# A fused retention and SwiGLU kernel: other places for the first weight loads and for one value load, and the first group's down-projection in three passes over w_out

## The chip, the cores and the metric

The kernel runs on one core of one Trainium2 chip. The metric is the device time of one execution in microseconds (us). The engines of the core have each an instruction queue that is worked off in order: TensorE (PE, with its weight loads shown apart as PEld), VectorE (DVE), ScalarE (ACT), GpSimd (POOL) and SyncE (SP). Transfers are issued from the queues of GpSimd, SP and ScalarE and are carried out by 16 DMA engines. PSUM, which TensorE writes, has eight banks, numbered 0 to 7 here.

## What is computed

`q`, `k` and `v` are (4, 8, 768, 64): batch, heads, positions, head width. The first half is a recurrent retention, the second a feed-forward block on its output, with 512 = 8 x 64 features per token, 3072 tokens and 1536 hidden features.

```python
gamma = 1.0 - 2.0 ** (-5.0 - np.arange(H))
for t in range(S):
    state = gamma[None, :, None, None] * state + np.einsum('bhd,bhe->bhde', k[:, :, t], v[:, :, t])
    y[:, :, t] = (1 / np.sqrt(D)) * np.einsum('bhd,bhde->bhe', q[:, :, t], state)
x = y.transpose(0, 2, 1, 3).reshape(B * S, H * D)

xn = x / np.sqrt(np.mean(x * x, axis=-1, keepdims=True) + 1e-6) * rms_g
g = xn @ w_gate
out = (g * (1 / (1 + np.exp(-g))) * (xn @ w_val)) @ w_out
```

Inputs and output are float32.

## The kernel before

The 768 positions are cut into six chunks of 128. In each chunk the four batches make two pairs, 0 and 1. The recurrence is done chunk by chunk: inside a chunk as a masked product of `q` and `k` (`a_ps`, then `am`) with the values, and across chunks through a state per batch and head. A chunk's rows are normed (`rstd` is a power of the mean square, on GpSimd; `xn` is the normed row), transposed to features by tokens (`xnT`), and go as a group of 512 tokens through the feed-forward: `gv` makes the gate and value products of some of the twelve 128-column blocks of `w_gate` and `w_val`, applies SiLU on ScalarE (`sg`) and multiplies on VectorE into `hT`; `down` multiplies `hT` with the twelve row blocks of `w_out` and stores a batch's 128 rows.

The order of instructions is written out by hand: each engine's queue holds its instructions in the order in which the program names them. TensorE works for the group of one chunk while the attention of the next chunk is put between its blocks.

The start is special, since all weights have to be fetched while the first chunk is computed. Weights, `q` and `k` are converted from float32 to bfloat16 by the transfer itself, and these transfers are issued by GpSimd. `load_w(n0, n1)` (line 83) loads blocks n0 to n1 of both weights as two transfers, `load_pair(c, p, n)` (line 93) one of `q`, `k`, `v` of pair p in two transfers of 64 partitions, `load_wo` (line 88) four row blocks of `w_out`. GpSimd's queue at the start is: `q` and `k` of pair 0, index patterns (lines 133 to 135), the second half of pair 0's `v`, `q` and `k` of pair 1, the positions `pos_p` and `pos_n` (lines 140 to 143), `ya_p` (line 195, from the positions), then blocks 0 and 1, blocks 2 and 3 (lines 569 and 570), the power of pair 0 (line 603), blocks 4 to 7, the decayed values of pair 0 (`vp_pair`, line 608), blocks 8 and 9, and the power of pair 1 (line 633). The `v` of pair 1 is issued from SP (line 587) after the first masked product.

ScalarE's queue there is: eight exponentials for the mask, the cast of pair 0's `v` (`vb`), the decays (`decays`, line 206: `vd_p`, `vd_n`, then `yd_p`, which reads `ya_p`, then `yd_n`), the copy of `g_bc` out of PSUM (line 593), the squares of pair 0 (line 330), two copies of pair 1's transposed `q`, and pair 0's `xn` (line 352). The copies of pair 1's transposed `k` are VectorE's (lines 604 and 605). The cast of pair 1's `v` (line 625) stands between the second and the third block's `sg`.

PSUM banks are given out by `bank` (line 65). Up to the end of chunk 1's start it takes them from a list written by hand (`first`), then from a rotation over eight banks (`order`). Once `split[0]` is true, tiles of the feed-forward turn over banks 4 to 7 and all others over banks 0 to 3. A bank is given to its next tile when the readers of its last tile are done. Before the change `split[0]` becomes true at line 723, ahead of the second group's feed-forward.

The first group's down-projection (lines 682, 692, 693 and 709) runs a batch at a time, twelve matmuls of 512 columns into one bank, with the second chunk's attention between the batches. The end of that stretch reads:

```python
    down(0, 1)
    down(0, 2)
    t_dma(2, 0)
    for n, e in (("q", "a"), ("k", "v")):
        for a in range(2):
            tp(1, 1, n, a, e)
```

and goes on with the transposes and products of pair 1 of chunk 1 (`x_pe`, `ap`), and `down(0, 3)`.

Of the kernel before, what the change touches and what calls it, by code (L numbers as in the profile page):

```python
# [8 lines left out]
F32 = mybir.dt.float32  # L9
# [7 lines left out]
def kernel(  # L17
# [11 lines left out]
    nc = tc.nc  # L29
    ctx.enter_context(tc.manual_schedule())  # L30

    B, H, S, D = q.shape
    C = 128
    NCH = S // C
    NHP = H // 2
    DM = H * D
    DFF = moe_w_gate.shape[1]
    KS = DM // 128
    NFF = DFF // 128
# [5 lines left out]
    work = ctx.enter_context(tc.tile_pool(name="work", bufs=4))  # L45
# [17 lines left out]
    split = [False]  # L63

    def bank(name, dtype=F32, ffn=False, i=None):
        if i is None and split[0]:
            i = turn[ffn] % 4 + 4 * ffn
            turn[ffn] += 1
        elif i is None and first:
            i = first.pop(0)  # L70
        elif i is None:
            i = order[0]
            order.append(order.pop(0))
        return psum.tile([128, 512 if dtype == F32 else 1024], dtype, name=name, tag=f"p{i}")
# [3 lines left out]
    wo_b = const.tile([128, NFF, DM], BF16, name="wo_b")  # L78
# [4 lines left out]
    def load_w(n0, n1, *kinds):  # L83
        sl = slice(n0 * 128, n1 * 128)
        for i in kinds or (0, 1):
            nc.gpsimd.dma_start(out=(wg_b, wv_b)[i][:, :, sl], in_=(wg_v, wv_v)[i][:, :, sl])
# [4 lines left out]
    U = {}  # L91

    def load_pair(c, p, n, batches=(0, 1), eng=None, after=None):
        u = U.setdefault((c, p), {})
        if n not in u:
            if n == "v":
                u[n] = work.tile([128, H, 2 * D], F32, name="v2f", bufs=3)
            else:
                u[n] = work.tile([128, H, 2 * D], BF16, name=n + "2b", bufs=4)
        for b in batches:  # L100
            i = (eng or nc.gpsimd).dma_start(out=u[n][b * 64:b * 64 + 64], in_=pair_v[n][c, 2 * p + b])  # L101
            if after is not None:
                tc.add_manual_dep(i.ins, after.ins.name, SYNC_DEP, reason="transfer order")

    def load(c, b, names="qkv"):
        u = U.setdefault((c, b), {})
        for n in names:
            if n == "v":
                x = work.tile([128, H, D], F32, name="v_f", tag="v_f", bufs=6)
                nc.gpsimd.dma_start(out=x, in_=unit_v[n][c, b])  # L110
            else:
                x = work.tile([128, DM], BF16, name=n + "b", bufs=8)
                nc.gpsimd.dma_start(out=x.rearrange("p (h d) -> p h d", h=H), in_=unit_v[n][c, b])  # L113
            u[n] = x
# [19 lines left out]
    for i in range(2):  # L134
        nc.gpsimd.iota(offp[i * 64:i * 64 + 64], pattern=[[-1, 2], [1, 2], [2, 64]], base=0, channel_multiplier=-2)
    load_pair(0, 0, "v", (1,))
    load_pair(0, 1, "q")
    load_pair(0, 1, "k")
    for i in range(2):
        nc.gpsimd.iota(pos_p[i * 64:i * 64 + 64], pattern=[[C, 2], [1, 2]], base=1, channel_multiplier=2,  # L140
                       allow_small_or_imprecise_dtypes=True)
    nc.gpsimd.iota(pos_n, pattern=[[C, NCH]], base=1, channel_multiplier=1,
                   allow_small_or_imprecise_dtypes=True)

    ones = const.tile([128, 512], BF16, name="ones")
    nc.vector.memset(ones, 1.0)  # L146
# [31 lines left out]
    def mask_exp(a):  # L178
        for i in range(2):
            for x in range(2):  # L180
                nc.scalar.activation(mask0[a][i][:, x], reach, AF.Exp, scale=lng[2 * (2 * a + x) + i], bias=lnscale)
# [39 lines left out]
    def copy(eng, out, in_):  # L221
        return (nc.scalar.copy if eng == "a" else nc.vector.tensor_copy)(out, in_)
# [16 lines left out]
    def tc_(c, p, n, a, eng):  # L239
        u = U[c, p]  # L240
        t = work.tile([128, 2, 2, 2, 64], BF16, name=n + "2T", tag=n + "T", bufs=8)
        copy(eng, t.rearrange("p x b e j -> p (x b e j)"), u["t_ps", n, a][:, :512])
        u[n + "T", a] = t
# [14 lines left out]
    def ap_mask(c, p, a, i):  # L258
        u = U[c, p]
        am = work.tile([128, 2, 2, 128], BF16, name="am2", tag="am", bufs=12)  # L260
        m = mask0[a][i] if c == 0 else causal_p[:, None, :].to_broadcast([128, 2, 256])
        u["mask", a, i] = nc.vector.tensor_tensor(  # L262
            out=am.rearrange("p x e t -> p x (e t)"),
            in0=u["a_ps", a][i].rearrange("p (x t) -> p x t", x=2), in1=m, op=ALU.mult)
        u["am", a, i] = am

    def v_cast(p):
        u = U[0, p]
        u["vb"] = work.tile([128, H, 2 * D], BF16, name="vb", bufs=2)
        nc.scalar.copy(u["vb"], u["v"])  # L270
# [87 lines left out]
    def begin(c):  # L358
        XT[c] = work.tile([128, KS, GT], BF16, name="xnT", bufs=2)
# [18 lines left out]
    def y1(p):  # L378
        u = U[1, p]
        u["y"] = [bank("y_ps") for _ in range(2)]  # L380
        for b in range(2):
            for hp in range(NHP):
                nc.tensor.matmul(u["y"][b][:, hp * 128:(hp + 1) * 128],
                                 u["qT", hp // 2][:, hp % 2, b].rearrange("p e j -> p (e j)"), st_d[p][:, b, hp],
                                 start=hp == 0, stop=False, skip_group_check=True)
        for h in range(H):
            hp, i = h // 2, h % 2
            for e in range(2):
                for b in range(2):
                    r = slice(b * 64, b * 64 + 64)  # L390
                    nc.tensor.matmul(u["y"][b][:, h * D:h * D + D], u["am", hp // 2, i][r, hp % 2, e, :],
                                     u["vp"][r, h, e * D:e * D + D], start=False,
                                     stop=h == H - 1 and e == 1, skip_group_check=True)

    def y1_out(p):
        u = U[1, p]
        x = work.tile([128, 2, NHP, 2, D], F32, name="x", tag="x", bufs=2)
        u["x"] = x.rearrange("p b a i d -> p b (a i d)")
        for b in range(2):
            nc.vector.tensor_tensor(  # L400
                out=u["x"][:, b].rearrange("p (h d) -> p h d", h=H), in0=u["y"][b].rearrange("p (h d) -> p h d", h=H),
                in1=yd_p[:, :, None].to_broadcast([128, H, D]), op=ALU.mult)
# [115 lines left out]
    HT = {}  # L518
# [22 lines left out]
    def store(eng, c, b, m, o_sb):  # L541
        if c < 2:
            for e in range(2):
                eng.dma_start(out=out_e[c, b, e][:, m], in_=o_sb[e * 64:e * 64 + 64, m])
        else:
            eng.dma_start(out=out_v[c, b][:, m], in_=o_sb[:, m])

    def down(c, b):
        ps = bank("o_ps", ffn=True)
        for n in range(NFF):  # L550
            nc.tensor.matmul(ps, HT[c][:, n, b * C:(b + 1) * C], wo_b[:, n, :], start=n == 0, stop=n == NFF - 1)  # L551
        o_sb = work.tile([128, DM], F32, name="o_sb", bufs=3)
        nc.scalar.copy(o_sb, ps)  # L553
        store(nc.sync, c, b, slice(0, DM), o_sb)

    def down_last(c, b):
        o_sb = work.tile([128, DM], F32, name="o_sb", bufs=3)
        for i in range(2):
            m = slice(i * 256, i * 256 + 256)
            ps = bank("o_ps", ffn=True)  # L560
            for n in range(NFF):
                nc.tensor.matmul(ps[:, :256], HT[c][:, n, b * C:(b + 1) * C], wo_b[:, n, m],  # L562
                                 start=n == 0, stop=n == NFF - 1)
            copy("av"[i], o_sb[:, m], ps[:, :256])
            store(nc.scalar if i == 0 else nc.sync, c, b, m, o_sb)


    begin(0)
    load_w(0, 2)
    load_w(2, 4)  # L570

    mask_exp(0)
    mask_exp(1)
    heat(11)
# [9 lines left out]
    for a in range(2):  # L584
        for i in range(2):
            ap_mask(0, 0, a, i)
    load_pair(0, 1, "v", eng=nc.sync, after=U[0, 0]["mask", 0, 0])
    v_cast(0)

    g_ps = bank("g_bc_ps")  # L590
# [11 lines left out]
    eps0(0)  # L602
    power(0, 0)
    tc_(0, 1, "k", 0, "v")
    tc_(0, 1, "k", 1, "v")
    load_w(4, 6)
    load_w(6, 8)
    vp_pair(0, 0)
# [70 lines left out]
    gv(0, 11, 12, 0, GT)  # L679
    load(2, 0)  # L680
    y1(0)
    down(0, 0)
    y1_out(0)
    square(1, 0, 0)
    square(1, 0, 1)
# [3 lines left out]
    load(2, 1)  # L689
    vp_pair(1, 1)  # L690
    load(2, 2)
    down(0, 1)
    down(0, 2)
    t_dma(2, 0)
    for n, e in (("q", "a"), ("k", "v")):
        for a in range(2):
# [9 lines left out]
            ap_mask(1, 1, a, i)  # L706
    load(2, 3)
    t_dma(2, 1)
    down(0, 3)

    def run(steps, after):
        for i, step in enumerate(steps):
# [7 lines left out]

    steps = [L(gv, 1, n, n + 2, t, t + 256) for t in (0, 256) for n in range(0, NFF, 2)]
    steps += [L(down, 1, b) for b in range(B)]
    split[0] = True
    run(steps, {
        0: [L(y1, 1), L(y1_out, 1), L(kvp, 1, 1)],
        1: [L(square, 1, 1, 0), L(square, 1, 1, 1), L(rstd, 1, 1), L(state1, 1)],
# [18 lines left out]
    for c in range(2, NCH):  # L745
# [6 lines left out]
        after = {}  # L752
        if d < NCH:
            after = {
                0: [L(begin, d)],
                1: [L(values, d, 0), L(vp, d, 2), L(vp, d, 3)],
                2: [L(y_out, d, 0, 0)] + [L(load, d + 1, 0)] * more,
                3: [L(y_out, d, 0, 1)] + [L(state_add, d, 0)] * more,
                4: [L(square, d, 0, 0)] + [L(load, d + 1, 1)] * more,
                5: [L(a_pair, d, 1), L(a_mask, d, 2, 0), L(square, d, 0, 1), L(rstd, d, 0)]  # L760
                   + [L(state_cast, 0)] * more,
                6: [L(a_mask, d, 2, 1), L(norm, d, 0, 0), L(x_dma, d, 0, 0)]
# [40 lines left out]
```

## Time and profile before

| what | value |
|---|---|
| median of 13 runs | 239.54 us (238.3 to 247.33) |
| the profiled execution's own time | 238.3 us |
| its span on the core | 236.5 us |
| TensorE busy | 225.2 us, 95% of the span |
| VectorE, ScalarE, GpSimd busy | 54%, 37%, 49% |
| granted TensorE clock | full in every slice |
| read from HBM, written to it | 28.32 MB, 6.29 MB |
| TensorE busy from 17.2 to 22.7 us | 3.93 of 5.50 us |
| TensorE busy from 28.0 to 46.6 us | 18.34 of 18.60 us |
| TensorE busy from 46.6 to 59.3 us | 12.60 of 12.70 us |

A timeline line has the start and the length in us, the engine, the line of the kernel, the operation, what is written and read, how many instructions were merged (x), and in brackets how long the engine was idle before it and what ended that. A line of the chain of waits has start, length and what was running. A line on transfers has what is written and read, the issuing queue, the number of transfers, the size as stored, and the median time from issue to landing. "PE", "DVE", "ACT" and "POOL" are TensorE, VectorE, ScalarE and GpSimd.

### The profile page before, as it was taken

What the parts mean: (1) busy time and instruction counts of PE and PEld (TensorE: products, weight loads), DVE (VectorE), ACT (ScalarE), POOL (GpSimd) and SP (SyncE); (2) the same over time, 40 slices, a digit from 0 to 9 for tenths busy, and PEclk for the clock granted to TensorE, in tenths of its full rate; (3) what the DMA queues carried; (4) which work ended last, traced back from release to release, by engine and by line L of the source; (5) the groups of instructions that cost most, each with busy time, mean ns of one, the idle gap of its engine ahead of it and who ended that gap; (6) DMA issues with size and microseconds to landing.
All of it is one profiled execution on the core that took longest, in us unless ns stands there. A gap on an engine that the chain in (4) does not pass through costs nothing.

```text
span 236.5 us, 5411 instructions
## 1 busy us (share of the span) xinstructions
PE 225.2 (95%) x2198; PEld 137.2 (58%) x2223; DVE 127.7 (54%) x222; ACT 87.5 (37%) x176; POOL 115.7 (49%) x150
## 2 busy tenths in 40 slices
PE   6787999999999999999999999999999999999993
PEld 2455775545898854684544684544674444854443
DVE  3775644827486585736956246957155742243300
ACT  2865634242443333235332325332325241433221
POOL 8976799559699923963918704907001010000000
PEclk9999999999999999999999999999999999999999
DMA  8999999999999999596999994994600205100022
GB/s 104 165 192 200 187 175 183 192 196 228 135 201 154 184 144 186 109 204 89 111 138 170 92 167 131 141 174 111 182 21 0 44 3 162 60 3 0 0 89 90
DMA packets 83306, 30.24 MB, mean 128 GB/s; under 512 B 69521, under 2 KB 78993, under 8 KB 83282
## 3 DMA queue, kind: packets, MB, share of 16 engines
q0 software_dynamic: 51328, 16.52, 67.9%
q1 hardware_dynamic: 31280, 13.25, 30.1%
q8 instruction: 17, 0.28, 0.5%
q10 hardware_dynamic: 674, 0.14, 0.3%
q14 instruction: 7, 0.06, 0.1%
HBM read 28.32 MB, written 6.29 MB: 146 GB/s over the span
## 4 chain that ended last, share of the span: by engine, by line
PE 87%; DMA 5%; DVE 3%; POOL 2%; issue 2%; DVEq 0%; POOLq 0%
PE v_ps L532 25%; PE o_ps L551 25%; PE g_ps L532 25%; DMA wv_b<-in_moe_w_val_dram 3%; DMA k2b<-in_k_dram 2%; PE y_ps L505 2%; PE a_ps L460 2%; DVE am L262 1%; PE y_ps L489 1%; PE t_ps L234 1%; PE o_ps L562 1%; PE kv_ps L498 1%; PE a_ps L255 1%; POOL q2b L101 1%; PE x_ps L365 1%
## 5 line engine op out<-in xcount | busy, mean ns | idle before, releaser
L537 DVE TENSOR_TENSOR hT<-sg,v_ps 128x512 bf16<-128x512 bf16 (+1 forms) x76 | 49.9, 657 | 73.9 <-PE v_ps L532 70.7
L532 PE MATMUL v_ps<-xnT,wv_b 128*128 128x256 bf16 (+1 forms) x427 | 74.9, 309 | 1.3 <-DMA wv_b<-in_moe_w_val_dram 0.9
L532 PE MATMUL g_ps<-xnT,wg_b 128*128 128x256 bf16 (+1 forms) x415 | 73.5, 307 | 1.3 <-DMA wg_b<-in_moe_w_gate_dram 0.7
L536 ACT ACTIVATE sg<-g_ps 128x512 bf16<-128x512 f32 (+1 forms) x76 | 43.6, 575 | 81.0 <-PE g_ps L532 76.1
L551 PE MATMUL o_ps<-wo_b,hT 128*128 128x512 bf16 x268 | 60.8, 379 | 0.4
L532 PEld LDWEIGHTS <-wv_b 128*128 128x128 bf16 x428 | 41.7, 98 | 22.2 <-DMA wv_b<-in_moe_w_val_dram 1.5
L532 PEld LDWEIGHTS <-wg_b 128*128 128x128 bf16 x428 | 40.3, 98 | 20.9 <-DMA wg_b<-in_moe_w_gate_dram 0.9
L551 PEld LDWEIGHTS <-hT 128*128 128x128 bf16 x276 | 26.5, 98 | 31.5
L429 POOL TENSOR_SCALAR m<-ms 128x2 f32<-128x2 f32 x10 | 2.2, 220 | 68.1 <-ACT xsq L424 68.1
L553 ACT COPY o_sb<-o_ps 128x512 f32<-128x512 f32 x23 | 13.4, 583 | 43.4 <-PE o_ps L551 43.4
L437 DVE SCALAR_TENSOR_TENSOR xn<-x,rstd,g_bc 128x512 bf16<-128x512 f32 x20 | 20.2, 1038 | 12.9 <-POOL rstd L345 12.9
L469 DVE TENSOR_TENSOR am<-a_ps,causal 128x512 bf16<-128x512 f32 x32 | 20.8, 678 | 0.0
L443 POOL TENSOR_TENSOR vp<-v_f,vd_n 128x512 bf16<-128x512 f32 x16 | 20.1, 1278 | 0.0
L113 POOL DMA_DIRECT2D qb<-in_q_dram x16 | 15.0, 938 | 0.6 <-DMA wo_b<-in_moe_w_out_dram 0.6
L424 ACT ACTIVATE xsq<-x 128x512 bf16<-128x512 f32 x20 | 12.4, 623 | 7.7 <-DVE x L415 7.7
L113 POOL DMA_DIRECT2D kb<-in_k_dram x16 | 14.4, 898 | 1.6 <-DMA wo_b<-in_moe_w_out_dram 1.6
L110 POOL DMA_DIRECT2D v_f<-in_v_dram x16 | 14.7, 918 | 0.6 <-DMA q2b<-in_q_dram 0.6
L415 DVE TENSOR_TENSOR x<-y_ps,yd_n 128x512 f32<-128x512 f32 x16 | 10.8, 683 | 0.6 <-PE y_ps L505 0.6
L219 PE MATMUL hot<-ones 128*128 128x512 bf16 x22 | 7.8, 456 | 1.5 <-DVE ones L146 1.4
L275 POOL TENSOR_TENSOR vp<-v2f,vd_p 128x1024 bf16<-128x1024 f32 x4 | 7.7, 1932 | 0.1
L345 POOL TENSOR_TENSOR rstd<-m,mhalf 128x2 f32<-128x2 f32 x10 | 7.2, 719 | 0.8
L101 POOL DMA_DIRECT2D q2b<-in_q_dram x8 | 5.8, 738 | 0.8 <-POOLq L787 0.8
(92 smaller groups left out, 154.3 us busy)
## 6 DMA issues: line engine op xcount, KB each, us to landing
v_f<-in_v_dram POOLq DMA_DIRECT2D x16, 256.0 KB, 7.3
out_dram<-o_sb SPq DMA_DIRECT2D x15, 256.0 KB, 2.3
out_dram<-o_sb SPq DMA_DIRECT2D x17, 128.0 KB, 4.9
qb<-in_q_dram POOLq DMA_DIRECT2D x16, 128.0 KB, 6.8
kb<-in_k_dram POOLq DMA_DIRECT2D x16, 128.0 KB, 7.3
wg_b<-in_moe_w_gate_dram POOLq DMA_DIRECT2D x6, 256.0 KB, 8.0
wv_b<-in_moe_w_val_dram POOLq DMA_DIRECT2D x6, 256.0 KB, 8.7
wo_b<-in_moe_w_out_dram POOLq DMA_DIRECT2D x3, 512.0 KB, 9.5
```

Of the source, the lines that this page charges most:

```text
L110: nc.gpsimd.dma_start(out=x, in_=unit_v[n][c, b])
L113: nc.gpsimd.dma_start(out=x.rearrange("p (h d) -> p h d", h=H), in_=unit_v[n][c, b])
L415: nc.vector.tensor_tensor(out=x[:, :, :, i, :], in0=u["y"][i].rearrange("p (b a d) -> p b a d", b=2, a=NHP), in1=yd_n[:, c, i][:, None, :, ...
L424: nc.scalar.activation(xsq, u["x"][:, b], AF.Square, scale=1.0 / math.sqrt(DM), accum_out=u["ms_"][:, b:b + 1])
L437: nc.vector.scalar_tensor_tensor(out=u["xn"][b], in0=u["x"][:, b], scalar=u["rstd"][:, b:b + 1], in1=g_bc, op0=ALU.mult, op1=ALU.mult)
L443: nc.gpsimd.tensor_tensor(out=x, in0=U[c, b]["v"], in1=vd_n[:, c, :, None].to_broadcast([128, H, D]), op=ALU.mult)
L469: nc.vector.tensor_tensor(out=x, in0=u["a_ps"][i].rearrange("p (a t) -> p a t", a=NHP), in1=causal[:, None, :].to_broadcast([128, NHP, 128 ...
L532: nc.tensor.matmul(x[:, o:o + w], wt[:, s, n * 128:(n + 1) * 128], XT[c][:, s, t0:t1], start=s == 0, stop=s == KS - 1)
L536: nc.scalar.activation(sg[:, :m], ps[0][:, :m], AF.Silu)
L537: return nc.vector.tensor_tensor(out=HT[c][:, n0:n1, t0:t1], in0=sg[:, :m].rearrange("p (n t) -> p n t", t=w), in1=ps[1][:, :m].rearrange( ...
L551: nc.tensor.matmul(ps, HT[c][:, n, b * C:(b + 1) * C], wo_b[:, n, :], start=n == 0, stop=n == NFF - 1)
L553: nc.scalar.copy(o_sb, ps)
```

## The change

In GpSimd's queue, block 0 of both weights is loaded ahead of pair 1's `q`, and block 1 as well as blocks 2 and 3 after pair 1's `k`, which itself comes after the positions. The loads of blocks 0 to 3 behind `begin(0)` go away. Pair 1's `v` is no longer issued by SP after the first mask but by GpSimd behind the power of pair 0 and ahead of blocks 4 to 7. The second copy of pair 1's transposed `k` goes from VectorE to ScalarE.

`down_third(c, t, *bs)` does a third of a down-projection: for each batch it multiplies with four of the twelve row blocks of `w_out`. Each batch's bank stays open from the first third to the last, and the third third copies and stores. The first group's calls are the first third of all four batches, the second third of all four, the last third of batch 0, and, behind the products of pair 1 of chunk 1, the last third of batches 1 to 3. `split[0]` becomes true ahead of the first of them.

```diff
@@ -134,13 +134,16 @@
     load_pair(0, 0, "v", (1,))
+    load_w(0, 1)
     load_pair(0, 1, "q")
-    load_pair(0, 1, "k")
     for i in range(2):
         nc.gpsimd.iota(pos_p[i * 64:i * 64 + 64], pattern=[[C, 2], [1, 2]], base=1, channel_multiplier=2,
                        allow_small_or_imprecise_dtypes=True)
     nc.gpsimd.iota(pos_n, pattern=[[C, NCH]], base=1, channel_multiplier=1,
                    allow_small_or_imprecise_dtypes=True)
+    load_pair(0, 1, "k")
+    load_w(1, 2)
+    load_w(2, 4)
...
+    DP = {}
+
+    def down_third(c, t, *bs):
+
+        for b in bs or range(B):
+            if t == 0:
+                DP[b] = bank("o_ps", ffn=True)
+            for n in range(4 * t, 4 * t + 4):
+                nc.tensor.matmul(DP[b], HT[c][:, n, b * C:(b + 1) * C], wo_b[:, n, :], start=n == 0, stop=n == NFF - 1)
+            if t == 2:
+                o_sb = work.tile([128, DM], F32, name="o_sb", bufs=3)
+                nc.scalar.copy(o_sb, DP[b])
+                store(nc.sync, c, b, slice(0, DM), o_sb)
...
     begin(0)
-    load_w(0, 2)
-    load_w(2, 4)
...
-    load_pair(0, 1, "v", eng=nc.sync, after=U[0, 0]["mask", 0, 0])
     v_cast(0)
...
     tc_(0, 1, "k", 0, "v")
-    tc_(0, 1, "k", 1, "v")
+    tc_(0, 1, "k", 1, "a")
+    load_pair(0, 1, "v")
     load_w(4, 6)
...
     y1(0)
-    down(0, 0)
+    split[0] = True
+    down_third(0, 0)
     y1_out(0)
...
-    down(0, 1)
-    down(0, 2)
+    down_third(0, 1)
+    down_third(0, 2, 0)
     t_dma(2, 0)
...
-    down(0, 3)
+    down_third(0, 2, 1, 2, 3)
...
-    split[0] = True
     run(steps, {
```

## The prediction

> **What bounds the kernel now.** I read the page first, then the chain of waits, then the timelines of GpSimd, ScalarE and TensorE in the two stretches that the change touches (5 to 28 us and 46 to 60 us), and the times to landing of single transfers.
>
> ```profile
> span 236.5 us, 5411 instructions
> PE 87%; DMA 5%; DVE 3%; POOL 2%; issue 2%; DVEq 0%; POOLq 0%
> ```
>
> TensorE carries the chain that ended last. What is not TensorE lies almost wholly in the first 30 us, and the chain of waits shows where:
>
> ```profile
> 14.09 0.18 DVE ms L340
> ...
> 14.41 0.72 POOL rstd L345
> 15.13 0.73 POOL wg_b L86
> 15.86 8.06 DMA wv_b<-in_moe_w_val_dram
> 23.96 0.61 PE v_ps L532 x4
> ```
>
> The loads of weight blocks 4 and 5 are issued behind the first power on GpSimd, and 8.06 us later they let TensorE go on. This is a full transfer queue more than a long transfer. Landing is issue plus time to landing: the last `k` piece of pair 1 lands at 7.92 + 4.8 = 12.7, `wv` of blocks 2 and 3 at 11.93 + 9.3 = 21.2, `wg` and `wv` of 4 and 5 at 15.09 + 7.5 = 22.6 and 15.86 + 8.1 = 23.9. From 12.7 to 21.2 four weight transfers and two of `v` land. A weight transfer (256 KB) takes 23.9 - 22.6 = 1.35 us, so a `v` takes (8.55 - 4 x 1.35) / 2 = 1.6. The four `q` and `k` pieces of pair 1 (128 KB, rows of 256 bytes) follow the `v` that landed at 5.24 + 4.2 = 9.45: 3.2 / 4 = 0.8 each. With these three prices the queue can be laid out anew. TensorE in the same stretch:
>
> ```profile
> 18.51 0.60 PE L532 MATMUL v_ps<-xnT,wv_b 128*128 128x256 bf16 x4
> 19.76 0.61 PE L532 MATMUL g_ps<-xnT,wg_b 128*128 128x256 bf16 x4 [0.66 <-DMA wg_b<-in_moe_w_gate_dram]
> 21.29 0.61 PE L532 MATMUL v_ps<-xnT,wv_b 128*128 128x256 bf16 x4 [0.91 <-DMA wv_b<-in_moe_w_val_dram]
> ...
> 22.70 0.64 PE L290 MATMUL y_ps<-vb,am 64*128 64x64 bf16 x32
> ```
>
> It loses 0.66 and 0.91 us on weights of blocks 2 and 3; that is what the reordered loads can remove.
>
> **Part 1, GpSimd's queue.** Starts follow each other by 0.74 us for weight transfers and 0.67 for `q` and `k` pieces. From 5.92: two of `load_w(0, 1)` to 7.4, two `q` to 8.75, the iotas to 9.35 (before 9.27, so `exponents()` on VectorE stays in place), two `k` to 10.75, then four weight transfers to 13.7. Only there stands the instruction that no hunk shows: `ya_p` (line 195), which ran ahead of the weights.
>
> ```profile
> 9.22 0.47 POOL L195 TENSOR_TENSOR ya_p<-pos_p,lngs 64x8 f32<-64x8 f32 x2
> 9.64 0.83 POOL L86 DMA_DIRECT2D wg_b<-in_moe_w_gate_dram  x1
> ```
>
> It now ends at 13.7 + 0.47 = 14.17 and not at 9.69. ScalarE reads it at line 209, in the middle of its own order:
>
> ```profile
> 11.13 0.29 ACT L209 ACTIVATE yd_p<-ya_p,lnscale 128x8 f32<-128x8 f32 x1
> ...
> 11.55 0.57 ACT L593 COPY g_bc<-g_bc_ps 128x512 f32<-128x512 f32 x1
> 12.78 0.60 ACT L330 ACTIVATE xsq<-y_ps 128x512 bf16<-128x512 f32 x1 [0.66 <-PE y_ps L290]
> ...
> 15.16 0.69 ACT L352 ACTIVATE xn<-y_ps,rstd 128x512 bf16<-128x512 f32 x1 [0.73 <-POOL rstd L345]
> ```
>
> `yd_p` goes from 11.13 to 14.2 (+3.1). Behind it stand `yd_n`, the copy of `g_bc`, the squares and the copies of `q2T`. The 0.66 us for which the squares waited covers part: they start at 15.2, 2.4 late. TensorE waits too, since the first transposes of pair 1 take the bank of `g_bc` (bank 0 in the hand-written list): 12.7 becomes 15.2. The sum of squares is read at 15.9; VectorE's own half was ready at 14.0, so `eps0` runs at 15.95 where it ran at 14.09: +1.85, and the power ends at 16.99 instead of 15.13. On ScalarE `q2T` (15.8 to 16.85) and the `k2T` copy that the change gives it (0.5) now stand ahead of `xn`: 17.3, which is 2.1 later than 15.16. So the first gate matmul goes from 17.20 to 19.3.
>
> **Part 2, what that gives back.** The queue laid out anew from 9.45: eight pieces of 0.8 (two `load_w(0, 1)`, four `q` and `k`, two `load_w(1, 2)`) and two of 1.35: blocks 0 to 3 are all there at 18.55, before 19.3. The two waits of 0.66 and 0.91 are gone, and four blocks of 0.87 end at 22.8, where they ended at 22.6. I took half-width blocks at the row of `q` and `k`, whose 256-byte rows they share; at half a wide transfer each (0.68) blocks 0 to 3 would be there 0.5 earlier, to no use.
>
> Then `v` of pair 1 is late. On SP's queue it was issued at 10.58 and 11.23 and had landed by 20.3; `vb` was cast at 20.34. Now GpSimd issues it behind the power, at 16.95 and 17.62. By the queue alone it lands at 18.55 + 2 x 1.6 = 21.75. But issue to landing is nowhere under 4.0 us in these loads, and for a `v`:
>
> ```profile
> v2f<-in_v_dram POOLq DMA_DIRECT2D x1, 256.0 KB, 4.2
> ```
>
> so the first half lands at 16.95 + 4.2 = 21.15 and the second 1.6 later, at 22.75: the queue runs dry for a while, as nothing stood in it behind block 3. I take 22.75, because a `v` on GpSimd's queue is the same transfer. The cast (1.05) ends at 23.8, the second pair's values start at 23.85 instead of 22.70 (+1.15), and behind the cast ScalarE still owes two `sg`, so that the squares and the second power come 1.3 late. The transposes of pair 1 (26.63) carry that on: **+1.3 us**. Weights 4 and 5 land at 22.75 + 2.7 = 25.45 against 23.9; the block that needs them moves to 24.5 and waits 0.9 for the second half, but two blocks end by 26.9 and the transposes wait for the norm until 27.9, which hides it. Bounds: +0.3 if `v` lands by the queue alone (values at 22.85, the squares 0.5 behind), +2.4 if nothing of the 2.1 and the further tail is given back. From 28 us on TensorE is busy 18.34 of 18.60 us, so there is nothing to absorb it.
>
> By the Trainium skill ("DMA: Bandwidth & Descriptors", section "Anatomy of one DMA - SWDGE (gpsimd) path") one such transfer costs about 2.0 us fixed plus its bytes at 436 GB/s, an estimate of 2.6 us for 256 KB against the 4.2 of the row; by that the queue, not the latency, would set the landing, and this part would come to +0.3. I hold with the row.
>
> TensorE idles about 2.4 us ahead of the first transposes of pair 1. The profile grants full clock in every slice, and shows no such gap behind the first matmuls. The skill's "TensorE: Matmul & The Clock Gate" (section "Why this matters for your kernels") asks for gaps under about 3 us; no run here shows what a longer one does.
>
> **Part 3, the down-projection by thirds.** The number of matmuls is the same, 36 ahead of the transposes of pair 1 of chunk 1 and 12 behind. `wo` is not late now: its last third lands at 35.88 + 11.2 = 47.1, and at 0.216 us each (four 512-column matmuls end in 1.03, of which the first takes 0.38) its first matmul came at 46.64 + 8 x 0.216 = 48.4. That cover of 1.3 us stays, as loads and TensorE move together. So the thirds remove nothing.
>
> But four banks (4 to 7) now stay open across the block at 54.5, and the other tiles turn over banks 0 to 3: four `t_ps`, two `x_ps`, four `a_ps`.
>
> ```profile
> 54.99 0.61 PE L234 MATMUL t_ps<-ident,k2b 128*64 128x128 bf16 x16
> 55.53 0.62 PE L365 MATMUL x_ps<-ident,xn 128*128 128x128 bf16 x8
> 56.08 0.64 PE L255 MATMUL a_ps<-q2T,k2T 64*64 64x128 bf16 x32
> 56.66 2.76 PE L551 MATMUL o_ps<-wo_b,hT 128*128 128x512 bf16 x11
> ```
>
> `x_ps` needs the `q2T` copies out of banks 0 and 1 (ScalarE, 55.10 to 56.18), so its second half runs at 56.2, not 55.8. The second pair of `a_ps` needs banks 0 and 1 again, that is both `xnT` copies on VectorE, the second of which then runs 56.65 to 57.05. It starts at 57.1 and ends at 57.4 instead of 56.7: **+0.7 us**, bounds 0 (copies faster than I place them) and +1.2 (both waits in full). Bank 7 holds `y` of the first pair; its reader (VectorE, 46.86 to 48.14) is done before the fourth accumulation starts at 49.2. Three stores move behind two DMA transposes on SP; the next ones there (64.43) slip by about two stores, 2.5 us, ahead of a use past 79.
>
> **Sum.** The profiled execution took 238.3 us (span 236.5). 238.3 + 1.3 + 0.7 = 240.3. It is the fastest of 13; their median is 239.54, 1.24 higher, so I predict 241.5.
>
> **Rivals.** (a) *The queue decides, not its issue* (the other side: not slower). The first 30 us move the same bytes in any order; if `v` starts as block 3 ends, its second half lands at 21.75, the values start at 22.85 and the front costs +0.3, with the banks hidden behind copies +0.1. Time 239.9. For: the queue is backed up to 30 us. Against: nothing is left in it at 18.55, 1.6 us after `v`'s issue. It decides if `v`'s second half lands by 21.7. (b) *The weight waits really go* (0.66 + 0.91 of TensorE time): 237.9. For it `v` would have to land by 20.3 as before, and ScalarE not to wait for `ya_p`; both speak against it. (c) *Nothing is given back*: `v` lands later still, since its issue waits on the power, and the 2.1 us reach the transposes whole with both bank waits: 239.5 + 2.4 + 1.2 = 243.1. (d) *The thirds don't do what they say*: as costed above, the wait that they shorten isn't there; this is in the forecast.
>
> **How the numbers follow.** Forecast 0.60 (own range 240.5 to 242.6), (a) 0.18, (b) 0.13, (c) 0.09. About 0.5%, 1.2 us, is what a measurement here can tell from no change. Slower: nearly all of the forecast and (c), 0.67; same: (a) and the forecast's low end, 0.20; faster 0.13. The range runs from (a)'s lower half to beyond (c), 238.9 to 243.5, and leaves out (b).
>
> **What would show it.** Right: `ya_p` near 13.7 behind four weight loads, `yd_p` above 14, the first gate matmul near 19.3 with no wait on weights of blocks 1 to 3, `vb` waiting for `v2f` to about 22.7, and an idle half microsecond between `x_ps` and `a_ps` near 58. Wrong: `yd_p` still at 11.1; `vb` cast before 21.5; no wait in the block of transposes; or the second transposes of `xn` no later than 26.7.

## The result, and the profile after

The changed kernel took 241.72 us (median of 11 runs, 241.04 to 248.64) against 239.91 us for the kernel before (48 runs beside it): a ratio of 1.0088 [1.0058, 1.0118], slower by 2.1 us by the ratio and 1.8 by the medians. The forecast was 241.5.

The execution profiled with this result was a disturbed one (span 242.8 us), so the lines below are of a second profile of the same changed kernel, whose run took 241.62 us, close to the median. First its page: the span, and the shares of the chain that ended last.

```profile
span 239.5 us, 5408 instructions
...
PE 83%; POOL 6%; DVE 3%; DMA 2%; ACT 2%; issue 2%; POOLq 0%; DVEq 0%
```

TensorE had 87% of the chain and has 83%; GpSimd went from 2% to 6%. The chain of waits between 14 and 25 us says what stands there now (start, duration, engine, output, line):

```profile
14.29 0.21 POOL ya_p L198
14.52 0.30 ACT yd_p L212
...
15.09 0.43 ACT g_bc L606
...
16.46 0.72 POOL rstd L348
17.17 0.71 POOL v2f L101
17.88 5.46 DMA v2f<-in_v_dram
23.36 1.05 ACT vb L273
```

Before, the chain at this place ran through the loads of weight blocks 4 and 5 (8.06 us on `wv_b`). Now the chain that the profile infers runs through `ya_p`, which waits for its turn behind four weight loads, from there through ScalarE to the first power, and only then to the issue and the landing of `v`. Its last link has to be read with care: kernels below that issue `v` 1.7 us earlier have it only 0.2 us earlier, so the queue sets the landing, and not the issue. TensorE's timeline of the same stretch (start, duration, operation, and in brackets the idle time before it with its releaser):

```profile
15.57 1.07 PE L237 MATMUL t_ps<-ident,q2b 128*64 128x128 bf16 x16 [2.55 <-ACT g_bc L606]
...
20.62 0.60 PE L535 MATMUL g_ps<-xnT,wg_b 128*128 128x256 bf16 x4 [0.24 <-ACT xnT L225]
...
24.46 0.64 PE L293 MATMUL y_ps<-vb,am 64*128 64x64 bf16 x32 [0.18 <-ACT vb L273]
...
28.41 0.64 PE L368 MATMUL x_ps<-ident,xn 128*128 128x128 bf16 x8 [0.33 <-ACT xn L355]
```

Between 20.62 and 24.28 the eight groups of blocks 0 to 3 follow each other every 0.44 us: the weight waits of 0.66 and 0.91 us are gone, as the reordered loads can have it. But the first gate matmul comes 3.42 us later than before (17.20), the second pair's values 1.76 later (22.70), the transposes of its `xn` 1.78 later (26.63). Of each, 0.27 us is a later start of this execution as a whole. Three stretches of this profile (start:end and length, busy time of TensorE, of its weight loads, VectorE, ScalarE and GpSimd, then the granted clock, the DMA share and GB/s) show what the gap of 2.55 us brought with it:

```profile
12.00:14.00 2.00, 0.72 (x17) 0.45 (x17) 1.49 (x4) 0.00 (x0) 2.00 (x4) 1.00 1.52 151
14.00:16.00 2.00, 0.43 (x10) 0.43 (x10) 0.22 (x2) 1.48 (x5) 0.41 (x2) 0.70 1.39 122
16.00:18.00 2.00, 2.00 (x29) 1.53 (x27) 1.07 (x3) 1.65 (x5) 1.54 (x3) 0.50 1.36 179
```

The clock falls to one half (from 14.79 to 18.20, 3.41 us), so that `t_ps` takes 1.07 us where it took 0.64. And the queue, which is busy all along, moves 151, 122 and 179 GB/s where the kernel before moved 159, 219 and 213. From 14 to 16 us these are about as many packets (868 against 848), but small ones: 752 of the 868 are under 512 bytes, and 22 of the 848. The second place is the block of transposes in chunk 1:

```profile
56.33 0.64 PE L237 MATMUL t_ps<-ident,q2b 128*64 128x128 bf16 x16
...
57.56 0.87 PE L368 MATMUL x_ps<-ident,xn 128*128 128x128 bf16 x8
58.37 1.00 PE L258 MATMUL a_ps<-q2T,k2T 64*64 64x128 bf16 x32
59.52 2.54 PE L567 MATMUL o_ps<-wo_b,hT 128*128 128x512 bf16 x11 [0.16 <-issue]
61.90 1.04 PE L535 MATMUL g_ps<-xnT,wg_b 128*128 128x256 bf16 x8
```

From `t_ps` to the next gate matmul it takes 61.90 - 56.33 = 5.57 us; before, 59.26 - 54.52 = 4.74. The same work is in it (11 recorded `o_ps` matmuls in both); `x_ps` and `a_ps` stretch from 0.62 and 0.64 to 0.87 and 1.00, as they wait for banks. The chain of waits has the copies that they wait for:

```profile
57.03 0.98 ACT q2T L225 x2
...
58.05 0.40 PE x_ps L368 x4
...
58.48 0.44 DVE xnT L225
...
58.95 0.41 PE a_ps L258 x15
```

`x_ps` does not read `q2T`, nor `a_ps` the `xnT`: it is the bank that the copy has to empty. This adds 0.83 us. Together the shift against the kernel before is 2.64 us behind this block, and it stays there up to 100 us: nothing later takes it back. (The profile before was the fastest of its 13 runs, 1.24 us under their median; this one lies at the median. That is why the traces stand further apart than the medians.)

### The profile page after: what moved, and what is told of

Read it like the earlier page. It is cut to its first block, busy times and chain, and to the rows that moved or that the text cites. A ratio compares the mean times of both kernels' runs of the same rounds, so it can differ in the third digit from the quotient of the medians.

```text
span 242.8 us, 5408 instructions
## 1 busy us (share of the span) xinstructions
PE 228.8 (94%) x2198; PEld 139.6 (57%) x2223; DVE 127.7 (53%) x221; ACT 88.1 (36%) x177; POOL 118.7 (49%) x154
## 4 chain that ended last, share of the span: by engine, by line
PE 81%; DMA 7%; POOL 6%; ACT 1%; issue 1%; DVE 1%; SPq 0%; POOLq 0%; DVEq 0%
PE v_ps L535 24%; PE g_ps L535 23%; PE o_ps L554 20%; PE o_ps L567 4%; DMA kT<-kb 4%; DMA wv_b<-in_moe_w_val_dram 3%; PE a_ps L463 2%; PE y_ps L508 2%; POOL wg_b L86 1%; POOL q2b L101 1%; POOL k2b L101 1%; PE o_ps L579 1%; PE y_ps L492 1%; POOL wv_b L86 1%; POOL v2f L101 1%
## 5 line engine op out<-in xcount | busy, mean ns | idle before, releaser
L535 PE MATMUL v_ps<-xnT,wv_b 128*128 128x256 bf16 (+1 forms) x427 | 75.7, 312 | 0.7 <-DMA wv_b<-in_moe_w_val_dram 0.4
L535 PEld LDWEIGHTS <-wv_b 128*128 128x128 bf16 x428 | 42.2, 99 | 21.7 <-DMA wv_b<-in_moe_w_val_dram 0.7
L554 PEld LDWEIGHTS <-hT 128*128 128x128 bf16 x228 | 22.2, 99 | 26.3 <-issue 0.3
L556 ACT COPY o_sb<-o_ps 128x512 f32<-128x512 f32 x19 | 11.1, 583 | 34.1 <-PE o_ps L554 34.1
L113 POOL DMA_DIRECT2D kb<-in_k_dram x16 | 14.3, 896 | 1.7 <-DMA wo_b<-in_moe_w_out_dram 1.7
L222 PE MATMUL hot<-ones 128*128 128x512 bf16 x22 | 9.4, 535 | 1.7 <-DVE ones L149 1.4
```

Of the source, the lines that this page charges most:

```text
L535: nc.tensor.matmul(x[:, o:o + w], wt[:, s, n * 128:(n + 1) * 128], XT[c][:, s, t0:t1], start=s == 0, stop=s == KS - 1)
```

## The experiments

All were timed in five rounds beside the kernel before. "Front" is what the change does up to 28 us, "thirds" what it does to the down-projection.

**The change again**, for a profile at its usual time and a second ratio.

> The changed kernel itself, for a profile beside those of its parts. Every theory expects the ratio 1.009 again. Theory A (GpSimd's queue holds up ya_p, TensorE idles 2 us before 15.5 us, and its clock is halved for 3.4 us behind that) expects yd_p above 14 us, an idle time of 2.0 to 2.2 us before the transposes of pair 1's q, and a granted clock of 0.5 from about 16.8 to 20.2 us. If the gap alone costs and the halved clock was that one run's accident (theory B), the clock is full in this profile.

Measured: 241.81 us, ratio 1.0067 [1.0040, 1.0095]; its profile is the one above. The gap and the halved clock are there again, the gap longer than expected (2.55 us) and the halved clock 2.0 us earlier (from 14.79).

**`ya_p` ahead of the weights.** The change, with `ya_p` given back its place, and `k` and the weights put behind its loop:

```diff
     nc.gpsimd.iota(pos_n, ...)
-    load_pair(0, 1, "k")
-    load_w(1, 2)
-    load_w(2, 4)
...
+    load_pair(0, 1, "k")
+    load_w(1, 2)
+    load_w(2, 4)
```

> ya_p stands ahead of pair 1's k and the weights in GpSimd's queue; all else as changed. Theory A: the gap of 2.1 us and the halved clock go away, the value load of pair 1 is issued at about 15.2 and lands by 21.8, and what is left is the bank waits and at most 0.3 us of the front: ratio to before 1.003 to 1.005 (+0.7 to +1.2 us). Rival C (the value load behind the power costs, not ya_p): the second pair's values still start over 1 us late and the ratio stays at 1.007 or more. Rival D (only the thirds cost): ratio 1.008 to 1.009 as changed.

Measured: 243.61 us, ratio 1.0121 [1.0063, 1.0178]; its six runs lie in two groups, 241.8 to 242.1 and 245.1 to 245.6. The gap did not go. It is 1.82 us long and now waits for `k2b`, which lands at 15.3 behind block 0 and `q` (14.3 with the prediction's 0.8 us for each piece); the clock is halved behind it from 15.9 to 19.3, and the values start at 24.25. So the edit exchanged one late operand of pair 1 for another, and could not tell whether `ya_p` mattered. The profiled execution is of the upper group, with one more wait of 2.05 us, for a transposed `xn`, at 107 us; what puts some runs of this kernel there is open.

**The two halves apart.** The front alone (the four `down` calls and `split` as before), and the thirds alone (the front as before):

```diff
-    down_third(0, 0)
+    down(0, 0)
...
-    down_third(0, 1)
-    down_third(0, 2, 0)
+    down(0, 1)
+    down(0, 2)
...
-    down_third(0, 2, 1, 2, 3)
+    down(0, 3)
```

> The front of the change alone: the first group's down-projection goes batch by batch as before, with the split of the banks after it. Theory A: the transposes of the second pair's norm are 1.3 to 2.2 us late, ratio 1.005 to 1.008; the block at 55 to 57 us is as short as before (2.1 us from the first transposes to the down-projection). Rival D: ratio 1.000 to 1.001.

> The thirds of the down-projection alone, with the banks split ahead of them; the front as before. Theory A: nothing until 54 us, then the block of pair 1's transposes takes 0.7 to 1.1 us longer, ratio 1.003 to 1.0045. If the waits on banks are hidden later: 1.000 to 1.001. Rival D: 1.008.

Measured: the front alone 241.25 us, 1.0038 [1.0011, 1.0065]; the thirds alone 241.27 us, 1.0028 [0.9994, 1.0061]. Both ratios lie a little below what was expected. Their excesses add up to 0.0066 and the whole change's is 0.0067; with intervals of 0.003 to either side an agreement as close as this is chance. In the front alone the transposes of `xn` come 2.37 us late (about 0.5 of it a later start of the execution) and the block at 56 us takes 4.74 us as before. Its clock was halved for 6.83 us (13.65 to 20.48), twice as long as in the change. In the thirds alone the front has its old order (the values come 0.77 us later than in the kernel before, behind longer waits for weights in this execution), and the block takes 60.85 - 55.29 = 5.56 us. The two halves are separate losses. The thirds' own interval just takes in no change, so for them the trace (0.83 us, 0.35%) and the experiment with work between the waits, below, carry the reading.

**Two waits in the front, taken away one by one.** All three kernels are edits of the front alone. In the first, `k` and `ya_p` go ahead of all weights (the three `load_w` lines stand behind the loop of `ya_p`) and `v` stays on GpSimd's queue behind the power. In the second, `v` goes back to SP's queue (the last two lines that change) and the order of the loads stays. The third does both.

```diff
-    load_w(0, 1)
     load_pair(0, 1, "q")
+    load_pair(0, 1, "k")
...
-    load_pair(0, 1, "k")
-    load_w(1, 2)
-    load_w(2, 4)
...
+    load_w(0, 1)
+    load_w(1, 2)
+    load_w(2, 4)
...
+    load_pair(0, 1, "v", eng=nc.sync, after=U[0, 0]["mask", 0, 0])
...
-    load_pair(0, 1, "v")
```

> Front of the change alone, with pair 1's k and ya_p ahead of all weights in GpSimd's queue (block 0 and block 1 in transfers of their own, v of pair 1 behind the power). Theory A2 (TensorE's gap has two causes, ya_p and the late k, each enough by itself; take both away and it goes): no idle time over 0.7 us before the transposes of pair 1, clock full there, the first gate matmul at 17 to 17.5 us. What is left is the late v: it lands at 21.6 to 23, the second pair's values start at 23 to 24, ratio 1.001 to 1.004. Rival C (v alone costs): ratio 1.004 as in the front alone. Rival E (k and ya_p alone cost): ratio 1.000 or less.

> Front of the change alone, but with v of pair 1 issued from SP after the first mask, as before. Theory A2: the gap and the halved clock stay, gates start at 20 to 20.6 and four blocks end at about 24, so that the values start at about 24 all the same, now held by TensorE and not by v: ratio 1.002 to 1.004, within 0.001 of the front alone. Rival C: the values start by 22.9 and the ratio is 1.000 to 1.001.

> Both: k and ya_p early, and v from SP; of the front only the split of blocks 0 and 1 into transfers of their own and the second k2T copy on ScalarE are left. Theory A2 and both rivals: as before, ratio 0.998 to 1.001. If the narrow weight transfers cost by themselves (more transfers, rows of 256 bytes): the weights of blocks 2 and 3 land 0.5 to 1 us later than before and the ratio is 1.002 to 1.003.

Measured, with the front alone in the first row and the kernel before in the last:

| `k`, `ya_p` | `v` | ratio | first gate | values | transposes of `xn` |
|---|---|---|---|---|---|
| behind weights | GpSimd | 1.0038 [1.0011, 1.0065] | 21.61 | 25.20 | 29.00 |
| ahead | GpSimd | 1.0065 [1.0033, 1.0096] | 17.57 | 24.31 | 28.25 |
| behind weights | SP | 1.0079 [1.0047, 1.0111] | 21.68 | 25.26 | 29.07 |
| ahead | SP | 1.0003 [0.9973, 1.0033] | 17.41 | 22.99 | 26.91 |
| (before) | SP | 1 | 17.20 | 22.70 | 26.63 |

Either repair alone brings nothing that can be told from the front as it was, and both ratios (1.0065 and 1.0079) are above what was expected; both repairs together bring all of it back. That is the mark of two waits that lie side by side, each long enough by itself. In the rows with late `k` and `ya_p` the clock was halved for 6.83 us (13.6 to 20.5), so that their first gate matmul comes 1.0 us later than the change's 20.62; in the other rows it stayed full. With the early `ya_p` (ratio 1.0065) there is no gap at 13 us and the clock is full throughout, yet TensorE then waits for `v`:

```profile
23.21 1.04 ACT L273 CAST vb<-v2f 128x1024 bf16<-128x1024 f32 x1 [3.72 <-DMA v2f<-in_v_dram]
```

```profile
24.31 0.64 PE L293 MATMUL y_ps<-vb,am 64*128 64x64 bf16 x32 [2.09 <-ACT vb L273]
```

ScalarE sat idle for 3.72 us until `v2f` had landed, and TensorE 2.09 us for the cast. The power comes early here, and with it the issue of `v` on GpSimd (17.13 in the change):

```profile
15.46 1.42 POOL L101 DMA_DIRECT2D v2f<-in_v_dram  x2
```

Still its second half lands at 16.19 + 7.0 = 23.19, against 23.34 in the change; in the kernel with `ya_p` ahead of the weights, which issues it at 15.39, at 23.13. So `v` is late by its place in the queue behind blocks 0 to 3, not by waiting for the power. With `v` on SP (ratio 1.0079) `v` is there at 18.95 and nobody waits for it, but the gap of 2.69 us at 13 us is back, the clock is halved behind it, and TensorE comes to the values only at 25.26. With both repaired:

```profile
17.41 0.60 PE L535 MATMUL g_ps<-xnT,wg_b 128*128 128x256 bf16 x4 [0.24 <-ACT xnT L225]
...
22.99 0.64 PE L293 MATMUL y_ps<-vb,am 64*128 64x64 bf16 x32
```

Here the weight waits return too (0.31, 0.43 and 0.73 us between these two lines): the weights of the change were early only for a TensorE that came late.

**`ya_p` late by itself.** The last kernel (ratio 1.0003) with the six weight loads moved from behind the loop of `ya_p` to ahead of it, `k` and `v` left as they are there; the one edit that puts the prediction's first step alone to the test.

```diff
     nc.gpsimd.iota(pos_n, ...)
+    load_w(0, 1)
+    load_w(1, 2)
+    load_w(2, 4)
...
-    load_w(0, 1)
-    load_w(1, 2)
-    load_w(2, 4)
```

> The kernel with k and ya_p early and v from SP (as before in time), with ya_p alone put behind the six weight transfers, where the change has it. The step of the prediction by itself: ya_p ends above 14, yd_p waits for it, TensorE idles over 2 us before the transposes of pair 1's q, its clock is halved for 3.4 us or more behind that, four blocks end at 23.7 to 24.5 and the values start then instead of at 23.0: ratio 1.003 to 1.006. If the wait on ya_p is harmless when k and v are early (weights are waited for anyway): 1.000 to 1.001.

Measured: 240.69 us, 1.0051 [1.0029, 1.0073]. TensorE's timeline and the stretch behind the gap:

```profile
15.49 1.06 PE L237 MATMUL t_ps<-ident,q2b 128*64 128x128 bf16 x16 [1.41 <-ACT g_bc L607]
...
20.84 0.60 PE L535 MATMUL g_ps<-xnT,wg_b 128*128 128x256 bf16 x4 [0.24 <-ACT xnT L225]
```

```profile
15.41:18.82 3.41, 3.10 (x38) 2.04 (x42) 1.25 (x3) 2.87 (x7) 2.44 (x4) 0.50 1.28 203
```

The bank of `g_bc` holds the transposes as predicted, and here also the clock falls to 0.50 for 3.41 us. (The gap is shorter than expected: the clock was halved from 8.58 to 11.99 as well, and TensorE came later to the wait.) An instruction of 0.2 us, moved in a queue, costs 0.5% (1.2 us of 240) with all transfers in time. The values start at 24.42 and not at 22.99.

The lower clock is no accident of the profiled executions. One halved stretch of 3.41 us leaves a mean granted clock of 0.993 over the span. Of the twelve runs of this kernel, the twelve of the change and the twelve with `v` on SP, none has a mean clock of 0.996 or more. Of the twelve with both repaired nine have, and of the 99 runs of the kernel before 69.

**The gap filled.** The change with nine of the kernel's own `heat` matmuls (products of ones that nobody reads) put into the gap, behind the first pair's squares, to ask what the halved clock costs by itself:

```diff
     squares0(0)
+    heat(9)
```

> The changed kernel with nine more of the matmuls that are done for warmth alone (1.9 us) on TensorE behind the first pair's values, where it idles. The clock should stay full. Theory A2 (v's landing at 23.3 and the cast hold the second pair's values, the halved clock is hidden behind that): ratio within 0.0015 of the change, 1.006 to 1.009. Rival F (the halved clock is what costs in the front): 0.8 to 1.5 us less than the change, ratio 1.001 to 1.004.

Measured: 243.41 us (six runs, 241.57 to 250.96), 1.0129 [1.0085, 1.0173].

```profile
15.55 0.64 PE L237 MATMUL t_ps<-ident,q2b 128*64 128x128 bf16 x16 [0.30 <-ACT g_bc L606]
...
24.19 0.64 PE L293 MATMUL y_ps<-vb,am 64*128 64x64 bf16 x32 [0.80 <-ACT vb L273]
```

The clock stayed full, `t_ps` took 0.64 us again and the first gate matmul came at 19.74 and not 20.62: 0.88 us is what the halved clock cost there. None of it reaches the values (24.19 against 24.46), since `v` lets them start no earlier. But TensorE was free for them at 24.19 - 0.80 = 23.39, 0.69 us later than in the kernel before, of which 0.46 is a later start of this execution (`k`'s first transposes at 8.67 and not 8.21). So with a full clock the late `ya_p` is nearly made up by the weight waits that vanish; of the 1.43 us by which it alone delays the values above (24.42 against 22.99) about 1.0 is the halved clock, an estimate from 24.42 - 23.39. The ratio missed both expectations. The three runs with a mean clock of 0.996 or more have a median of 241.94 us, no better than the change; the span of the profiled one is 239.8 us, 0.3 over the change's. Why the other runs are longer is not settled.

**The thirds, with work between the waits.** The thirds alone, but with the last third of batch 1 put between `t_ps` and `x_ps` (behind the second transposes of `q` and `k`), and that of batch 2 ahead of `a_ps`, so that TensorE has something to do while the banks are copied out:

```diff
+    down_third(0, 2, 1)
...
     x_copy(1, 0, 1, "v")
+    down_third(0, 2, 2)
...
-    down_third(0, 2, 1, 2, 3)
+    down_third(0, 2, 3)
```

> Front as before; the thirds as in the change, but with the last third of batch 1 between the transposes of pair 1's q and k and those of xn, and the last third of batch 2 ahead of its masked products, so that TensorE has 0.87 us of matmuls in each of the two waits for banks. Bank theory: from the first transposes to the next group's first gate matmul it takes 4.75 us as before (5.6 in the thirds alone), ratio 0.999 to 1.001. If something else in the thirds costs (the later stores on SP, the open banks): 1.002 to 1.004 as in the thirds alone.

Measured: 240.04 us, 0.9990 [0.9954, 1.0026].

```profile
56.28 0.64 PE L234 MATMUL t_ps<-ident,q2b 128*64 128x128 bf16 x16
...
57.52 0.81 PE L564 MATMUL o_ps<-wo_b,hT 128*128 128x512 bf16 x3 [0.16 <-issue]
58.17 0.61 PE L365 MATMUL x_ps<-ident,xn 128*128 128x128 bf16 x8
58.61 1.03 PE L564 MATMUL o_ps<-wo_b,hT 128*128 128x512 bf16 x4
59.57 0.64 PE L255 MATMUL a_ps<-q2T,k2T 64*64 64x128 bf16 x32
...
61.02 1.04 PE L532 MATMUL g_ps<-xnT,wg_b 128*128 128x256 bf16 x8
```

`x_ps` and `a_ps` have their 0.61 and 0.64 us back, and the block takes 61.02 - 56.28 = 4.74 us, that of the kernel before to the hundredth. The loss was the wait for banks, and it goes when matmuls that need no new bank stand there. A gain from the thirds does not appear even so: there was no wait on `wo` to shorten.

**Two tries at a better kernel.** The first takes the weight waits of the kernel before from the other side: pair 1's values and squares go ahead of weight block 3, with two `heat` matmuls less; the hand-written list of banks follows.

```diff
-    gv(0, 3, 4, 0, 256)
...
     squares0(1)
+    gv(0, 3, 4, 0, 256)
...
-    heat(3, 2)
+    heat(1, 2)
```

> The kernel before, with the second pair's values and squares ahead of the fourth weight block instead of behind it, and one warming matmul instead of three ahead of its xn transposes. If the second pair's values, cast and norm are what the front hangs on (the reading of all runs so far), the values start at 21.7 to 21.9 instead of 22.7, the xn transposes at 25.6 to 26.0 instead of 26.6, ratio 0.996 to 0.998. If the weights' landing is (rival W), nothing moves: 0.999 to 1.001.

Measured: 239.74 us, 1.0007 [0.9978, 1.0036]: no gain. In its profile the values start at 23.89, after 1.26 us of waiting for `vb`. In that execution the clock was halved early on (8.5 to 11.9 us) and pair 1's first transposes came 1.5 us late, so the profile settles little beyond this: the values wait for the cast of `v` there, where before they waited for nothing.

The second is the whole change with all that was found mended: `k` and `ya_p` ahead of the weights, `v` on SP, the last thirds between.

> The whole change with both of its costs mended: k and ya_p ahead of the weights and v from SP as in the run that was as fast as before, and the last thirds of batches 1 and 2 between the transposes as in the run that covered the waits for banks. If the two parallel waits in the front (late k and ya_p, late v) and the waits for banks are the whole of the loss: first gate matmul at 17.2 to 17.6, values at 22.7 to 23.2, 4.75 us from pair 1's transposes to the next group's first gate matmul, ratio 0.998 to 1.002. If something else in the change costs: 1.003 or more.

Measured: 240.04 us, 1.0014 [0.9981, 1.0048]; the clock is full, the block takes 60.45 - 55.71 = 4.74 us, and the weights are waited for again (0.68, 0.71 and 0.72 us). The values start at 23.90, later than expected (22.7 to 23.2). The ratio leaves nothing of the change's loss that can be told from no change, to about 0.3%, and no version was faster than the kernel before.

## Why the prediction was right, step by step

The forecast (241.5, slower) came true, and 241.72 lies inside its own range. The late operands and the banks that it named are the ones that cost. But the term that sets the front, the landing of `v`, had the right size for a wrong reason, which is luck (step 4). Of its steps:

1. **GpSimd's queue.** Right. `ya_p` ends at 14.50 (forecast 14.17, and this execution starts 0.27 later).
2. **ScalarE, the bank of `g_bc`, the power.** Right in its chain: `yd_p` at 14.52 (14.2), squares at 15.42 (15.2), a gap of 2.55 us (2.4), the power's end at 17.18 (16.99). Mis-sized at its end: the first gate matmul came at 20.62, not 19.3. The forecast named the gap and priced its length, but not the halved clock behind it, which cost 0.88 us at that matmul. The Trainium skill ("TensorE: Matmul & The Clock Gate", section "Why this matters for your kernels") asks for gaps under about 3 us; 2.55 us and, with `ya_p` alone late, 1.41 us were followed by half clock, so here the measurement decides. The error was harmless in the sum, because `v` came later still; with `v` in time the halved clock is most of what the late `ya_p` costs.
3. **The weights of blocks 0 to 3.** Right that the two waits go and that the weights are there in time; the queue was mis-sized. Laid out at 0.8 us for a half-width piece, it should have had block 3 at 18.55; the last one landed at 13.19 + 7.8 = 21.0. From `v`'s first landing at 9.61 the same ten transfers took 11.4 us, not 9.1. Three of the four half-width pieces did land within 0.8 us of the transfer ahead of them, and the four pieces of `q` and `k` took 0.7 to 1.25 us each; but 2.46 us passed before the fourth half-width piece (`wv` of block 1, from 15.53 to 17.99), in the stretch of the lowest rate above. What held it up is open.
4. **`v` late.** Right in effect, wrong in its reason. The halves landed at 17.13 + 5.1 = 22.2 and 17.88 + 5.46 = 23.34; the forecast had 21.15 and 22.75. It held with a latency of 4.2 us over an empty queue. The queue was never empty: weights were moving until 21.0, and the halves follow 1.2 and 1.1 us after the transfer ahead of each (1.6 was forecast). Issuing `v` 1.7 us earlier gained 0.2 us. So it was rival (a)'s mechanism, the queue decides, but with a queue that ran 2.5 us later than rival (a) laid out, and hence, by luck, with about the forecast's price. Its condition (the second half by 21.7) failed by 1.6 us. The estimate from the Trainium skill's figure for one transfer ("DMA: Bandwidth & Descriptors", section "Anatomy of one DMA - SWDGE (gpsimd) path": 2.0 us and its bytes) stands on the same layout and missed in the same way.
5. **The sum of the front.** +1.3 was forecast, 1.78 - 0.27 = 1.51 us measured at the transposes of `xn`, within the bounds (+0.3 to +2.4). What the forecast did not see is its form: it told one chain, and there are two waits, either of which costs the whole: `v` by its place in the queue, `ya_p` mostly by the clock that falls behind its gap. The kernels with one repaired show this (1.0065 and 1.0079), and that with both (1.0003).
6. **The thirds.** Right: they remove nothing, and the banks cost 0.83 us (forecast 0.7, bounds 0 to 1.2). SP's next DMA transposes slipped by 7.3 us (64.43 to 71.69) instead of 2.5, and cost nothing that the trace shows.

Rival (b) was right that TensorE's weight waits vanish, and wrong that this is time: they turned into the wait for `v`. Rival (c) had 3.6 us of losses; 2.3 to 2.6 us show in the trace and 1.6 to 2.1 in the medians. The measured sum, 1.51 + 0.83 = 2.34 us, stands against 2.0 forecast.

## What to carry to other kernels

When a load is moved up in a queue, follow every small instruction behind it, through every engine that reads its result, to the bank or buffer that this holds back: here an operation of 0.2 us behind the loads cost 1.2 us, most of it by the clock that fell behind the gap. When a load is issued late into a queue that is still full, ask what stands ahead of it before pricing its latency. Where two edits of a change each seem to cost the same loss, remove them one by one and both together; a repair that gains nothing by itself may only stand beside a second wait. And a loop that keeps more banks open needs matmuls that want no bank put between the tiles that now turn over the rest.

## What the hardware showed that was not expected

The granted clock fell to one half after gaps of only 2.55, 1.82 and 1.41 us behind the first matmuls, for 3.41 us each time, and at gaps of 2.26 (front alone) and 2.69 us (`v` on SP) for 6.83 us. A gap of 2.09 us at 22 us (early `ya_p`, `v` on GpSimd) left it full, and filling the first gap down to 0.30 us kept it full. From one change of the clock to the next it is always a whole number of stretches of 3.41 us: 10.24, then 3.41 in the change. That length agrees with the Trainium skill's free-running window of 3413 ns ("TensorE: Matmul & The Clock Gate", section "What's actually happening"), so where a gap falls may count as much as its length; no run here separated the two.

In three profiles the clock was also halved early ahead of any gap of the change (8.5 to 11.9 us in that with the earlier values, 8.58 to 11.99 in that with `ya_p` alone late, 8.86 to 19.1 in that with thirds between). The kernel before has runs with a lower clock too: the 30 of its 99 with a mean under 0.996 have a median of 240.72 us, the others 239.48. Where in them it falls no trace shows.

In the full queue the issue of a load said little of its landing: `v`, issued 1.7 us earlier, landed 0.2 us earlier. And the rate in bytes went with the size of the packets: between 14 and 16 us about as many were moved as before, at 122 GB/s against 219.
